# A retention layer and a two-matrix block on one core: unit 3 is loaded earlier and turned by the DMA queue, k and v come by halves from unit 4 on

## The chip, the cores and the metric

The kernel runs on one core of a Trainium2 chip. The core has a matrix engine (TensorE, PE in the profile; PEld is its weight load), a vector engine (VectorE, DVE), a scalar engine (ScalarE, ACT), a general engine (GpSimd, POOL) and a queue engine (SyncE, SP) that issues most transfers. Each engine runs its own instructions in the order in which they were written; semaphores hold an instruction back until what it reads is there. The metric is the device time of one execution in microseconds (us), the median of several runs.

## The reference

Eight heads (H = 8) of width 64 (D) are processed for four batches (B = 4) of 768 tokens (S). Per head a 64 by 64 state decays and takes in the outer product of k and v; a token's output is its q times the state:

```python
gamma = 1.0 - 2.0 ** (-5.0 - np.arange(H, dtype=np.float32))
scale = 1.0 / np.sqrt(D)
for t in range(S):
    state = gamma[None, :, None, None] * state + np.einsum('bhd,bhe->bhde', k[:, :, t], v[:, :, t])
    y[:, :, t] = scale * np.einsum('bhd,bhde->bhe', q[:, :, t], state)
...
h = x @ w_in            # x: y as 3072 tokens by 512; w_in 512 by 2048
g = np.maximum(h, 0.0) + alpha * np.minimum(h, 0.0)
return (g @ w_out).astype(np.float32)   # w_out 2048 by 512
```

Inputs and the output are 32-bit floats.

## The kernel before

**Units and blocks.** The 3072 tokens are cut into 12 units of 256 tokens (three per batch), and two units make a block of 512 tokens; there are six blocks. A unit holds two chunks of 128 tokens, which lie on two halves of 64 partitions with two tokens (r = 0 and 1) per partition.

**A unit's retention.** `load` brings k, q and v (1.5 MB in all) from memory with DMAs issued by SP. `rescale` multiplies k and q by decay factors into 16-bit numbers (on POOL or DVE), `cast_v` turns v into 16 bits. q and k are then needed transposed (`kq`): `turn_pe` does it with 8 PE transposes and one ScalarE copy for each half of the heads, `turn_dma` with one transposing DMA issued by SP. `score_mm` multiplies k with q into two PSUM banks, `masks` (DVE) multiplies with the causal mask, `sum_mm` and `state_sum` / `state_copy` carry the state (PE, DVE, POOL, with copies on POOL or ACT), and `out_mm` adds the state's part (line 319) and the masked part (line 339). `take_y` writes the unit's output as 16-bit numbers.

**Two layouts of k and v.** Below `SPLIT` (6 before) one DMA brings a whole k or v, partition p holding tokens 2p and 2p+1 of a chunk in rows of 512 bytes (line 149). From `SPLIT` on four DMAs bring k and four bring v (line 143), each in rows of 256 bytes, so that r = 0 is the first half of a 128-token chunk and r = 1 the second. Then the matmuls for r = 1 need only the later 64 of 128 columns, in the scores (line 284) and in the output (line 339), and a mask is 384 wide instead of 512 (line 297 instead of 301). q is loaded the same way in both.

**A block's two products.** `ffn1` multiplies the block with w_in on PE (line 407), ScalarE takes the negative part (line 418) and DVE combines the two (line 420). `ffn2` multiplies with w_out (line 445, block 0 only); from block 1 on `ffn2_seven` does it with seven instead of eight block products (line 493), from sums of w_out (`w_sums`, line 378, one wide instruction and six narrower ones, on DVE) and sums of g (`g_sums`, line 391, on DVE).

**Order.** There is no planner: the order is written out by hand. `ffn1` and `ffn2` are generators that yield after each matmul, and `tick(gen, m)` puts m matmuls of one of them between other work. In the stretch that the change touches, `gen` is `ffn2` of block 0 and `half` is `ffn1` of block 1, whose first half (48 ticks) needs only unit 2 and whose second half needs unit 3 too. Weights come in four pieces each, from POOL's queue (`get_wi`, `get_wo`). `hold` lets the next load of `load` wait for an instruction that was put into `held`. `behind` lets a rescale on POOL wait for the last `w_sums` or `g_sums` on DVE. Buffers of k, q, v, `kdq`, `kq` and `vx` are threefold. SP's queue carries loads, the transposing DMAs and the stores of the output in one order, and each waits for the one before it to be issued.

Of the kernel before, what the change touches and what calls it, by code (L numbers as in the profile page):

```python
# [21 lines left out]
def kernel(  # L22
# [15 lines left out]

    SPLIT = 6
    U = 256
    UPB = S // U
    NU = B * UPB
# [42 lines left out]
    HF, HM = NFT // 2, d_model // 2  # L87
# [15 lines left out]
    held = []  # L103

    def behind(ins, other):
        tc.add_manual_dep(
            ins.ins,
            other.ins.name,
            mybir.DependencyInfo(
                mybir.DependencyClass.Sync, mybir.DependencyReason.DATA  # L110
            ),
            reason="one engine of two at the second read port",
        )
# [52 lines left out]
    def rescale(eng, u, t, h0, h1):  # L166
        kdq = unit(u)[0]
        at = OQ if t else (O2 if u >= SPLIT else 0)
        return eng.tensor_tensor(  # L169
            out=kdq[:, t, :, h0:h1, :].rearrange("p r h d -> p h r d"),  # L170
            in0=staged[u]["kq"[t]][:, h0:h1, :].rearrange("p h (r d) -> p h r d", r=2),
            in1=tab[:, at + 2 * h0 : at + 2 * h1]
            .rearrange("p (h r) -> p h r", r=2)
            .unsqueeze(3)
            .to_broadcast([128, h1 - h0, 2, D]),
            op=MULT,
        )

    def cast_v(eng, u, h0=0, h1=H):
        o = unit(u)[2][:, h0:h1].rearrange("p h r d -> p (h r d)")  # L180
        i = staged[u]["v"][:, h0:h1].rearrange("p h x -> p (h x)")
        if eng is nc.scalar:
            eng.activation(out=o, in_=i, func=COPY, bias=0.0, scale=1.0)
        else:
            eng.tensor_copy(out=o, in_=i)  # L185
# [107 lines left out]
    def masks(u, hh, parts=(0, 1)):  # L293
        for a in parts:
            m2 = sbp.tile([128, 512], F16, tag=f"m2{a}{hh}", bufs=2, name=f"m2{a}{hh}")
            if u >= SPLIT:
                i = nc.vector.tensor_tensor(
                    out=m2[:, 0:384], in0=live[u, hh][a][:, 0:384], in1=mj, op=MULT
                )
            else:  # L300
                i = nc.vector.tensor_tensor(  # L301
                    out=m2.rearrange("p (r a i) -> p r a i", r=2, a=2),
                    in0=live[u, hh][a].rearrange("p (r a i) -> p r a i", r=2, a=2),
                    in1=mask.unsqueeze(2).to_broadcast([128, 2, 2, 128]),
                    op=MULT,
                )
            live[u, hh][a] = m2
        return i

    def out_mm(u, banks, evict=True):  # L310
        _, kq, vx = prepped[u]
        ys = [ps(banks[0], "y0"), ps(banks[1], "y1")]
        inter = [(u, c) in tgs for c in range(2)]
        assert inter == [u % UPB > 0, True]

        for c in range(2):
            for p in range(NP):
                if inter[c]:
                    nc.tensor.matmul(  # L319
                        out=ys[c][:, 128 * p : 128 * p + 128],  # L320
                        lhsT=tgs[u, c][:, p, :],
                        rhs=kq.rearrange("p (t r a) i -> p t r a i", t=2, r=2)[
                            :, 1, :, p, rows(c)
                        ],
                        start=(p == 0),
                        stop=False,
                        skip_group_check=True,
                    )
        for p in range(NP):
            m2s = live[u, p // 2]  # L330
            for r in range(2):
                for c in range(2):
                    for a in range(2):
                        o = ys[c][rows(a), 128 * p : 128 * p + 128]
                        at, n = 256 * r + 128 * (p % 2), 128
                        if u >= SPLIT and r == 1:
                            at, n = 256 + 64 * (p % 2), 64
                            o = o.rearrange("p (r i) -> p r i", r=2)[:, :, 32:64]
                        nc.tensor.matmul(  # L339
                            out=o,  # L340
                            lhsT=vx[rows(c), 2 * p + a, r, :],
                            rhs=m2s[a][rows(c), at : at + n],
                            start=(r == 0 and p == 0 and not inter[c]),
                            stop=(r == 1),
                            skip_group_check=True,
                        )
        live[u] = ys
        if evict:
            take_y(u, (0, 1))
# [20 lines left out]
    def w_sums(i, lo, hi):  # L370

        w = w_out_all.rearrange("p (k f) (j e) -> p k f j e", k=2, j=2)
        w12, w21, w22 = w[:, 0, lo:hi, 1, :], w[:, 1, lo:hi, 0, :], w[:, 1, lo:hi, 1, :]
        t1, t2, t3, t4 = (wsum[:, x, lo:hi, :] for x in range(4))
        o, a, b = (
            (t1, w12, w[:, 0, lo:hi, 0, :]), (t2, w22, t1), (t3, w22, w12), (t4, w21, t2)
        )[i]
        return nc.vector.tensor_tensor(out=o, in0=a, in1=b, op=SUB)
# [190 lines left out]
    def tick(gen, m=10**6):  # L569
        for _ in range(m):  # L570
            if next(gen, 1) == 1:
                return
# [8 lines left out]
    def get_wo(i):  # L581
        s = slice(4 * i, 4 * i + 4)
        return nc.gpsimd.dma_start(out=w_out_all[:, s, :], in_=wo[:, s, :])
# [88 lines left out]
    get_wo(1)  # L672
    rescale(G, 2, 1, 0, 4)
    rescale(G, 2, 0, 4, 8)
    rescale(G, 2, 1, 4, 8)
    cast_v(G, 2)
    out_mm(1, (4, 5), evict=False)
    take_y(1, (0,))
    take_y(1, (1,), V)
# [1 line left out]


    gen = ffn2(0, (0, 1, 2, 3), parts=4)
    half = ffn1(1, (6, 7, 4, 5, 4, 6, 0, 1, 2, 3, 0, 4, 5, 6, 7, 1), apart=12)
    tick(gen, 5)
    turn_pe(2, 0, 5)
    tick(gen, 5)
    score_mm(2, 0, (6, 7))
    held.append(masks(2, 0, (0,)))
    load(3, ("k0", "q0", "k1", "q1", "v"))  # L690
    masks(2, 0, (1,))
    turn_pe(2, 1, 4)
    tick(gen, 6)
    score_mm(2, 1, (6, 7))
    sum_mm(2, (5, 4))
    state(2, 0, G, "ga")
    masks(2, 1)
    held.append(get_wo(2))
    load(4)
    load(5)  # L700
    rescale(V, 3, 0, 0, 4)
    rescale(G, 3, 1, 0, 4)
    get_wo(3)
    rescale(V, 3, 0, 4, 8)
    rescale(G, 3, 1, 4, 8)
    cast_v(G, 3)
    w_sums(0, 0, HF)
    tick(gen, 9)
    out_mm(2, (4, 5))
    tick(gen, 7)  # L710
    tick(half, 24)
    turn_pe(3, 0, 6)
    tick(half, 8)
    turn_pe(3, 1, 7)
    tick(half, 16)
    tick(gen, 9)
    score_mm(3, 0, (4, 5))
    masks(3, 0)
# [7 lines left out]
    for f in (0, 4):  # L726
        for i in range(1, 4):
            gate = w_sums(i, f, f + 4)
    behind(rescale(G, 4, 1, 0, 8), gate)
    rescale(G, 5, 0, 0, 8)  # L730
    rescale(G, 5, 1, 0, 8)
    cast_v(G, 4)
    cast_v(G, 5)
    tick(gen, 8)
    out_mm(3, (6, 7))
    tick(gen)
# [6 lines left out]
    for n in range(1, NBLK):  # L743
        more = n + 1 < NBLK
        u0 = 2 * (n + 1)
        if n > 1:
            gen = ffn1(n, (7, 2, 3, 1, 0, 6, 5, 4, 7, 1, 0, 4, 5, 6, 7, 1))
            if more:
                for u in (u0, u0 + 1):
                    i = rescale(G, u, 0, 0, 8)  # L750
                    if u == u0:
                        behind(i, gate)
                    rescale(G, u, 1, 0, 8)
                    turn_dma(u)
                    cast_v(G, u)
                    if u + 2 < NU:
                        load(u + 2)
                    tick(gen, 8)
            tick(gen)
        gen = ffn2_seven(n, 0, 1) if more else ffn2_seven(n, (0, 3), 1, 2)  # L760
        if more:
            tick(gen, 8)
            sum_mm(u0, (2, 3))
            sum_mm(u0 + 1, (2, 3), half=1)
            score_mm(u0, 0, (4, 5))
            score_mm(u0, 1, (6, 7))
            state(u0, 0, G)
            masks(u0, 0)
            s01 = state_sum(u0, 1, G)
            masks(u0, 1, (0,))  # L770
            s10 = state_sum(u0 + 1, 0, G)
            masks(u0, 1, (1,))
            tick(gen, 8)
            state_copy(s01, "aa")
            state_copy(s10)
            tick(gen, 17)
            if n == 1:
                load(7)
            state(u0 + 1, 1, G)
            g_sums(n, 2, 0, HF)  # L780
            tick(gen, 15)
            out_mm(u0, (4, 5))
            score_mm(u0 + 1, 0, (6, 7))
            score_mm(u0 + 1, 1, (2, 3))
            masks(u0 + 1, 0)
            masks(u0 + 1, 1)
            gate = g_sums(n, 3, 0, HF)
            tick(gen, 32)
            out_mm(u0 + 1, (4, 5))
        else:  # L790
            tick(gen, 33)
            g_sums(n, 2, 0, HF)
            g_sums(n, 3, 0, HF)
        tick(gen)
# [30 lines left out]
```

## Time and profile before

The median is 202.07 us (three runs: 201.91, 202.07, 203.52). The profiled execution took 203.15 us.

| what | value |
|---|---|
| profiled execution, its span | 203.15 us, 201.4 us |
| PE busy, share of the span | 193.2 us, 96% |
| DVE busy | 155.3 us, 77% |
| ACT busy | 102.0 us, 51% |
| POOL busy | 85.1 us, 42% |
| granted clock of PE | full (1.00) |
| moved by DMA | 33.95 MB, mean 169 GB/s |

Busy time is what the profiler saw an engine work. A granted clock of 1.00 means that nothing slowed PE. A line of the timeline gives the start and the length in us, the engine, the line of the kernel, the operation, what it writes and reads, and how many instructions were merged; in brackets stands how long the engine sat idle before and who ended that.

### The profile page before, as it was taken

The page shows a single profiled execution, that of the slowest core. Times are in us where ns is not written, and L with a number is a line of the kernel's source. Part 1 is how long each engine was busy: PE and PEld are TensorE (multiplying, and loading weights), DVE is VectorE, ACT ScalarE, POOL GpSimd, SP SyncE. Part 2 cuts the span into 40 slices and gives each one's busy share as a digit, 9 for nine tenths or more (in the row PEclk, how much of TensorE's full clock was granted, in tenths as well). Part 3 has the DMA queues.
Part 4 walks back from the last instruction along what each step waited for, and adds up shares of the span by engine and source line. Part 5 has one row for each costly group of instructions (what it writes and reads, how often), then busy time and mean ns, then how long its engine had stood idle before and what let it go on. Part 6 is the DMA issues. An engine that isn't in the chain of part 4 may idle for free.

```text
span 201.4 us, 5574 instructions
## 1 busy us (share of the span) xinstructions
PE 193.2 (96%) x2325; PEld 129.0 (64%) x2325; DVE 155.3 (77%) x251; ACT 102.0 (51%) x170; POOL 85.1 (42%) x99
## 2 busy tenths in 40 slices
PE   6896999999999999999999999999999999999993
PEld 2455644577467778744788644788544888544882
DVE  7695887657799999189997389994489984589851
ACT  2455776348276433477354377334476255466321
POOL 6189029282459463970076950176920250000000
PEclk9999999999999999999999999999999999999999
DMA  6999999499999997998976499992570011300014
GB/s 170 312 230 148 205 251 260 136 245 198 339 344 136 215 222 180 240 277 221 213 188 162 157 178 240 198 225 87 175 160 0 3 53 55 107 0 0 14 41 156
DMA packets 77561, 33.95 MB, mean 169 GB/s; under 512 B 43217, under 2 KB 77025, under 8 KB 77537
## 3 DMA queue, kind: packets, MB, share of 16 engines
q1 hardware_dynamic: 73136, 29.37, 56.8%
q0 software_dynamic: 4224, 4.19, 13.4%
q8 instruction: 18, 0.29, 0.6%
q10 hardware_dynamic: 176, 0.04, 0.1%
q14 instruction: 7, 0.05, 0.1%
HBM read 27.31 MB, written 6.29 MB: 167 GB/s over the span
## 4 chain that ended last, share of the span: by engine, by line
PE 86%; DMA 6%; DVE 2%; POOL 2%; SPq 1%; issue 1%; ACT 0%; POOLq 0%
PE hps L407 41%; PE ox L493 16%; PE oy L493 11%; PE ops L445 7%; DMA win<-in_moe_w_in_dram 4%; PE y L339 3%; DMA vs<-in_v_dram 3%; PE y L319 2%; PE sca L284 2%; SPq L149 1%; PE st L229 1%; PE trb L199 1%; PE oz L493 1%; DVE gs L391 1%; POOL tf L255 1%
## 5 line engine op out<-in xcount | busy, mean ns | idle before, releaser
L407 PE MATMUL hps<-xT,win 128*128 128x512 f16 (+1 forms) x448 | 84.7, 349 | 1.6 <-DMA win<-in_moe_w_in_dram 1.6
L420 DVE SCALAR_TENSOR_TENSOR gt<-hm,oma,hps 128x512 f16<-128x512 f32 (+1 forms) x112 | 71.1, 668 | 10.2 <-ACT hm L418 4.9
L418 ACT ACTIVATE hm<-hps 128x512 f32<-128x512 f32 x96 | 57.2, 597 | 32.2 <-PE hps L407 29.7
L407 PEld LDWEIGHTS <-win 128*128 128x128 f16 x448 | 43.5, 98 | 40.2 <-DMA win<-in_moe_w_in_dram 1.7
L493 PEld LDWEIGHTS <-gs 128*128 128x128 f16 x320 | 31.0, 98 | 3.8
L255 POOL TENSOR_TENSOR tf<-ss,tab 128x256 f32<-128x256 f32 x16 | 12.2, 764 | 36.2 <-DVE ss L254 35.3
L493 PEld LDWEIGHTS <-gt 128*128 128x128 f16 x240 | 22.8, 98 | 4.6
L509 ACT ACTIVATE cu<-ox 128x512 f32<-128x512 f32 (+1 forms) x18 | 9.5, 527 | 29.3 <-PE ox L493 29.2
L169 POOL TENSOR_TENSOR kdq<-ks,tab 128x1024 f16<-128x1024 f32 (+1 forms) x10 | 17.3, 1729 | 15.6 <-DMA ks<-in_k_dram 8.4
L514 DVE TENSOR_TENSOR os<-oy,cu 128x512 f32<-128x512 f32 x14 | 9.6, 689 | 17.2 <-PE oy L493 13.5
L169 POOL TENSOR_TENSOR kdq<-qs,tab 128x1024 f16<-128x1024 f32 (+1 forms) x13 | 21.3, 1641 | 2.8 <-issue 1.9
L270 POOL CAST tg<-tf 64x256 f16<-64x256 f32 x27 | 13.2, 491 | 19.6 <-DVE tf L251 18.3
L493 PE MATMUL ox<-wsum,gs 128*128 128x256 f16 x160 | 19.1, 273 | 0.0
L362 ACT ACTIVATE xT<-y 128x512 f16<-128x512 f32 x23 | 15.7, 743 | 6.0 <-PE y L339 5.8
L445 PE MATMUL ops<-wout,gt 128*128 128x512 f16 x64 | 15.3, 380 | 0.0
L185 POOL CAST vx<-vs 128x1024 f16<-128x1024 f32 (+1 forms) x13 | 12.5, 971 | 4.1 <-DMA vs<-in_v_dram 4.1
L391 DVE TENSOR_TENSOR gs<-gt 128x1024 f16<-128x1024 f16 (+1 forms) x14 | 13.1, 934 | 0.3
L268 ACT ACTIVATE tg<-tf 64x256 f16<-64x256 f32 x13 | 5.3, 414 | 14.0 <-POOL tf L255 9.0
L205 ACT ACTIVATE kq<-trb 128x1024 f16<-128x1024 f16 x8 | 8.2, 1024 | 7.1 <-PE trb L199 7.0
L301 DVE TENSOR_TENSOR m<-sca,mi 128x512 f16<-128x512 f32 x12 | 8.2, 687 | 3.4 <-PE scb L284 3.4
L493 PE MATMUL ox<-wout,gt 128*128 128x256 f16 x80 | 10.4, 274 | 0.0
L445 PEld LDWEIGHTS <-gt 128*128 128x128 f16 x64 | 5.8, 98 | 6.0
(55 smaller groups left out, 190.7 us busy)
## 6 DMA issues: line engine op xcount, KB each, us to landing
out_dram<-os SPq DMA_DIRECT2D x21, 256.0 KB, 3.0
qs<-in_q_dram SPq DMA_DIRECT2D x8, 512.0 KB, 5.7
ks<-in_k_dram SPq DMA_DIRECT2D x24, 128.0 KB, 3.5
vs<-in_v_dram SPq DMA_DIRECT2D x24, 128.0 KB, 4.8
ks<-in_k_dram SPq DMA_DIRECT2D x8, 256.0 KB, 4.8
qs<-in_q_dram SPq DMA_DIRECT2D x8, 256.0 KB, 5.1
win<-in_moe_w_in_dram POOLq DMA_DIRECT2D x4, 512.0 KB, 7.8
wout<-in_moe_w_out_dram POOLq DMA_DIRECT2D x4, 512.0 KB, 8.1
```

Of the source, the lines that this page charges most:

```text
L169: return eng.tensor_tensor(out=kdq[:, t, :, h0:h1, :].rearrange("p r h d -> p h r d"), in0=staged[u]["kq"[t]][:, h0:h1, :].rearrange("p h ...
L185: eng.tensor_copy(out=o, in_=i)
L255: eng.tensor_tensor(out=t, in0=ss, in1=dec, op=MULT)
L270: nc.gpsimd.tensor_copy(out=o, in_=i)
L362: nc.scalar.activation(out=o, in_=i, func=COPY, bias=0.0, scale=1.0,)
L391: return nc.vector.tensor_tensor(out=o, in0=a, in1=b, op=op)
L407: nc.tensor.matmul(out=hps[:, f, :].rearrange("p (u t) -> p u t", t=U), lhsT=w_in_all[:, hp, 128 * (f0 + f) : 128 * (f0 + f) + 128], rhs=x ...
L418: nc.scalar.activation(out=hm, in_=hps, func=RELU, bias=0.0, scale=-1.0)
L420: nc.vector.scalar_tensor_tensor(out=gt[:, f0 + f, U * lo : U * hi], in0=hm[:, f, :], scalar=oma_sb[:, f0 + f : f0 + f + 1], in1=hps[:, f, :],
L445: nc.tensor.matmul(out=opss[tq], lhsT=gt[:, ft, 128 * tq : 128 * tq + 128], rhs=w_out_all[:, ft, :], start=(ft == 0), stop=(ft == NFT - 1),)
L493: nc.tensor.matmul(out=o[1][m], lhsT=lhs(f, m), rhs=rhs(f), start=(first and f == 0 and (m == 0 or o[0] is None)), stop=(f == HF - 1), ski ...
L514: nc.vector.tensor_tensor(out=so, in0=o[0], in1=t, op=ADD)
```

## The change

Six edits of the order of the program, and one number.

1. `SPLIT` goes from 6 to 4: units 4 and 5 load k and v by halves, with nine DMAs each instead of three, and use the narrower matmuls and masks.
2. Unit 3's loads are issued behind unit 2's last rescale (POOL) instead of behind unit 2's first mask (DVE). The third piece of w_out is issued right behind `cast_v` of unit 2, no longer later with the loads of unit 4 waiting for it.
3. Unit 3 is turned by `turn_dma` and not by two `turn_pe`; the loads of units 4 and 5 stand behind that in SP's queue.
4. The first 48 ticks of `half` run without a break, and its banks change with that.
5. The first, wide `w_sums` stands behind those ticks on DVE instead of ahead of them.
6. On POOL the casts of v of units 4 and 5 stand earlier among the rescales.
7. In the loop, the second mask of the second half of the heads stands ahead of the state's sum of the next unit.

```diff
-    SPLIT = 6
+    SPLIT = 4
...
-    rescale(G, 2, 1, 4, 8)
+    held.append(rescale(G, 2, 1, 4, 8))
+    load(3, ("k0", "q0", "k1", "q1", "v"))
     cast_v(G, 2)
+    get_wo(2)
...
-    half = ffn1(1, (6, 7, 4, 5, 4, 6, 0, 1, 2, 3, 0, 4, 5, 6, 7, 1), apart=12)
+    half = ffn1(1, (6, 7, 4, 5, 6, 7, 0, 1, 2, 3, 0, 4, 5, 6, 7, 1), apart=12)
...
-    held.append(masks(2, 0, (0,)))
-    load(3, ("k0", "q0", "k1", "q1", "v"))
-    masks(2, 0, (1,))
+    masks(2, 0)
...
-    held.append(get_wo(2))
-    load(4)
-    load(5)
     rescale(V, 3, 0, 0, 4)
     rescale(G, 3, 1, 0, 4)
     get_wo(3)
     rescale(V, 3, 0, 4, 8)
     rescale(G, 3, 1, 4, 8)
+    turn_dma(3)
+    load(4)
+    load(5)
     cast_v(G, 3)
-    w_sums(0, 0, HF)
     tick(gen, 9)
     out_mm(2, (4, 5))
     tick(gen, 7)
-    tick(half, 24)
-    turn_pe(3, 0, 6)
-    tick(half, 8)
-    turn_pe(3, 1, 7)
-    tick(half, 16)
+    tick(half, 48)
+    w_sums(0, 0, HF)
     tick(gen, 9)
     score_mm(3, 0, (4, 5))
...
+    cast_v(G, 4)
     behind(rescale(G, 4, 1, 0, 8), gate)
     rescale(G, 5, 0, 0, 8)
+    cast_v(G, 5)
     rescale(G, 5, 1, 0, 8)
-    cast_v(G, 4)
-    cast_v(G, 5)
...
             masks(u0, 1, (0,))
+            masks(u0, 1, (1,))
             s10 = state_sum(u0 + 1, 0, G)
-            masks(u0, 1, (1,))
```

## The prediction

> **What bounds the kernel now.** I read the page's busy shares first, then the chain that ended last, then PE's timeline around units 3 to 5, then SP's.
>
> ```profile
> span 201.4 us, 5574 instructions
> PE 193.2 (96%) x2325; PEld 129.0 (64%) x2325; DVE 155.3 (77%) x251; ACT 102.0 (51%) x170; POOL 85.1 (42%) x99
> PE 86%; DMA 6%; DVE 2%; POOL 2%; SPq 1%; issue 1%; ACT 0%; POOLq 0%
> ```
>
> PE carries the end: from 17.7 us on, when the first weights land, it has one idle stretch before its last matmul, and that is 0.43 us long. So a change is worth what it takes off PE's own work plus that stretch, less any new wait of PE. PE's timeline at the places touched:
>
> ```profile
> 45.52 0.62 PE L199 MATMUL trb<-mi,kdq 128*128 128x128 f16 x8
> 45.98 1.04 PE L407 MATMUL hps<-xT,win 128*128 128x256 f16 x8
> 46.85 0.61 PE L199 MATMUL trb<-mi,kdq 128*128 128x128 f16 x8
> 47.30 1.91 PE L407 MATMUL hps<-xT,win 128*128 128x256 f16 x16
> ...
> 66.87 1.04 PE L493 MATMUL ox<-wout,gt 128*128 128x256 f16 x8
> 74.72 0.41 PE L339 MATMUL y<-m,vx 64*64 64x128 f16 x15 [0.43 <-DVE m L301]
> 83.63 13.98 PE L407 MATMUL hps<-xT,win 128*128 128x512 f16 x64
> 156.25 1.07 PE L493 MATMUL ox<-wout,gt 128*128 128x256 f16 x8
> 171.99 1.24 PE L407 MATMUL hps<-xT,win 128*128 128x512 f16 x5
> ```
>
> See in it: the two groups of transposes of unit 3 (start to start 0.46 and 0.45 us), the one wait, and the same stretch of program twice. From the first `ox` of block 1 to the next block's `hps` (66.87 to 83.63) PE handles units 4 and 5 in the wide form; from 156.25 to 171.99 it handles units 10 and 11, which stand at the same places in their batch and run the same instructions, in the narrow form.
>
> SP's queue is what the change loads more:
>
> ```profile
> 47.78 0.37 SPq L149 DMA_DIRECT2D ks<-in_k_dram  x1
> 53.77 2.20 SPq L149 DMA_DIRECT2D vs<-in_v_dram  x1
> 59.05 0.62 SPq L459 DMA_DIRECT2D out_dram<-cu  x1
> 62.12 5.63 SPq L189 DMA_TRANSPOSE kq<-kdq  x2
> 67.84 2.75 SPq L143 DMA_DIRECT2D ks<-in_k_dram  x4
> 71.31 4.78 SPq L143 DMA_DIRECT2D vs<-in_v_dram  x4
> 76.80 2.66 SPq L143 DMA_DIRECT2D ks<-in_k_dram  x4
> 80.23 3.59 SPq L143 DMA_DIRECT2D vs<-in_v_dram  x4
> 95.56 2.84 SPq L189 DMA_TRANSPOSE kq<-kdq  x1
> 98.45 3.50 SPq L143 DMA_DIRECT2D ks<-in_k_dram  x4
> 102.67 4.63 SPq L143 DMA_DIRECT2D vs<-in_v_dram  x4
> ```
>
> Units 4 and 5 took 47.78 to 55.97 us to issue, whole. Halved loads take longer: unit 6 67.84 to 76.09 (8.25), unit 7 76.80 to 83.82 (7.02), unit 9 98.45 to 107.30 (8.85, the longest), unit 8 6.65 (the shortest).
>
> **The parts.**
>
> *Transposes on PE.* 16 leave the path: 0.46 + 0.45 = **0.91 us**. The two ScalarE copies (1.02 us each) lay beside PE.
>
> *Narrow units 4 and 5, and the moved mask.* The twin stretches give it at once: 16.76 us (83.63 - 66.87) against 15.74 us (171.99 - 156.25), so **1.02 us**. The 0.43 us wait is in that. I check that the wait can go: DVE's masks took 0.685 us and take 0.547 narrow (groups by form), so the four of unit 4 end 0.55 us sooner; the one that PE waited for also no longer stands behind a state's sum (0.33 us in the queue, and 0.22 us idle for POOL's product before it). It was 0.43 us late; it is then some 0.6 us early. The state's sum that now stands behind it feeds `out_mm` of unit 5 at 79.0 us, over 4 us later. In later blocks the same swap fills a DVE idle of 0.33 us (102.87) off the path.
>
> *Unit 3's loads.* Held behind POOL's last rescale of unit 2, which ends at 33.91, they start 2.75 us sooner than at 36.69. They now meet the rest of w_out's second piece (landed 36.1) and the third piece, issued at about 34.9. In the trace k's and q's second halves landed 6.0 and 6.7 us after the first issue; unit 2's loads beside weights took 10.4 and 11.2. The nearest row is the former, with a third piece also in flight, so I take 8 us for q's second half, landing near 42.0 (bounds 40.6 and 45.1). POOL, freed of the third piece's issue (0.81 us), rescales the first half of q at 40.1 and issues the fourth piece at 41.1, then rescales the second half by 43.1 us (1.04 us; it took 1.92 beside the wide `w_sums`, which moves away). Nothing on PE waits for a load here but through the next part.
>
> *The DMA turn of unit 3.* Issued at 43.1; the eight in the trace took 3.7 to 6.3 us to land, so kq is there at 46.8 to 49.4. PE wants it at 51.1 - 0.9 = 50.2. Cost nothing: 48 steps of `half` and nine of `gen` (42.9 to 51.1 us before) stand in front and hide it. If q lands at 45.1, the turn lands at up to 52.5, and PE waits 2.3 us. The fourth piece of w_out, wanted at about 52.5, landed 8.4 us after issue: 49.5.
>
> *Loads of units 4 and 5.* They stand behind that turn on SP, whose issue takes 1.3 to 2.8 us: start near 45.4, not 47.78. I take 8.25 + 7.02 = 15.3 us for the pair, the rows of the first pair behind a turn (bounds 13.3 and 17.7, twice the shortest and twice the longest). SP is done at 60.7. Behind that stand four stores (0.33 to 0.62 us when not held: 1.7 in all), so unit 4's turn is issued at 62.4, against 62.12 before; its rescale, gated by `w_sums`, is done at about 61.2 and is not last. It landed in 5.6 us before, others behind stores in 4.4 and 4.7; with 5.0 kq is there at 67.4. PE wants it (score of unit 4, 68.29 before) at 68.29 - 0.91 = 67.4. So the wait is about 0, and between -2.5 (turn issued at 61.2, landed in 3.7) and +3.7 us (17.7 for the pair, landed in 6.3) at the ends. I put **0.2 us** on the path, because the estimate sits on the edge and only lateness counts.
>
> [...]
>
> *v and the rest on SP.* v of unit 5 lands some 4.2 us after its last issue, near 64; its cast ends at 65.1, wanted at 66.9. The rescale of q behind it ends at 67, 1.2 us later than before, and unit 5's turn lands by 73, about when PE wants it (73.3, by the twin stretch). Unit 6's loads start 1 to 1.5 us later; in the stores ahead of unit 6's turn (83.92 to 86.44, they waited for DVE) there is that much room. Unit 7's turn landed at 101.9, PE wants it at 104.7 - 1.9 = 102.8. Cost nothing.
>
> *The wide sum and the casts.* `w_sums` (1.22 us) moves to about 49.6 on DVE, where before it had idle gaps of 0.52 and 0.84 us; the masks of unit 3 start 0.2 us behind PE, caught up in the second gap. POOL's cast of unit 4 (1.03 us) falls beside the last sums; beside POOL work such sums took 0.88 to 1.10 instead of 0.68 us, so up to 0.8 us is added on DVE. The sum that PE needs next, `gs` of block 1, ended at 70.97 and was wanted at 71.54: 0.57 us of slack. Cost 0 to 0.3; I take 0, as the ten last steps of `half` let DVE catch up (its 0.75 us a step on the last four against PE's 0.87).
>
> **Sum.** -0.91 - 1.02 + 0.2 = -1.73 us: the profiled execution would take 203.15 - 1.73 = 201.4. That one ran 1.08 us over the median; on the median's scale 202.07 - 1.73 = **200.3 us**, 0.86% less. About 1% (2 us) is what a measurement of this kernel can tell from no change.
>
> **Rivals.**
>
> *Unit 4's turn is late.* The loads of units 4 and 5 run as unit 6's and unit 9's did (17 us), or the first turn starts a microsecond late. PE waits 0.6 to 1.9 us at the first score of unit 4: 200.7 to 202.1. For it: the estimate has no margin, and before there was only 0.6 us (landed 67.7, wanted 68.29). Against it: the loads start 2.4 us sooner. Chance 0.25.
>
> *Slower: halves drag the whole queue.* Same place, decided by the pair's time: PE waits for 52.1 + P - 67.4, so from P = 17.2 us on the whole gain is gone, and at 17.7 with a turn of 6.3 us behind a backlog (as at 95.56) the wait is 3.7: 203.8. If the pair also shares the rings with w_out's fourth piece, still 0.5 MB, P reaches 19 and the time 205. Against it: no pair in the trace took more than 15.5. Chance 0.15, 0.09 of it over 1%.
>
> *Unit 3's turn is the late one.* q's second half lands at 45.1 as beside weights: PE waits up to 2.3 us at the first score of unit 3, and everything after shifts with it, so that unit 4's turn then costs little more: 201 to 202.6. Chance 0.1.
>
> *The change gives all of it.* No new wait at all: 200.1, and below 200.05 (over 1%) with a noise of 0.1 to 0.2 us. The forecast with its 0.2 us and this case together hold 0.5, of which 0.24 lies below 200.05.
>
> **How the numbers follow.** The forecast's own range is 199.8 to 200.7 (0.5); rivals reach on: to 202.1 (0.25), 202.6 (0.1) and 205 (0.15). Leaving 0.05 below and 0.12 above, the range is 199.8 to 203.0. Faster by over 1%: 0.27, with a little for waits that I overrate. Slower by over 1%: 0.1. Within: 0.63.
>
> **What would show it.** Right: no line 199 after 37 us; PE's stretch of block 1 close to 15.7 us; no wait on PE for the masks of unit 4. Unit 3's turn on SP near 43, landed before 50; loads of units 4 and 5 ending near 60.7; unit 4's turn landing near 67.4. Wrong: PE idle ahead of line 284 at 50 or 67 us, or ahead of line 493 at 70 us for `gs`, or SP still issuing halves after 62 us.

## The result, and the profile after

The changed kernel takes 207.49 us (median of six runs, 206.42 to 208.44) against 202.22 us (six runs of the kernel before, 201.91 to 203.52): a ratio of 1.0251, with a 95% interval of 1.0204 to 1.0298. It is slower. The forecast of 200.3 us and its whole range, up to 203.0, miss it. The profiled execution after took 207.50 us. Here and below a median is that of all executions of a kernel, while a ratio leaves out those that ran in a slower state, so the two need not agree.

The page of the kernel after, its span, busy times and the engines' shares of the chain that ended last:

```profile
span 205.8 us, 5554 instructions
PE 192.6 (94%) x2309; PEld 127.5 (62%) x2309; DVE 154.8 (75%) x251; ACT 100.3 (49%) x168; POOL 84.7 (41%) x99
PE 76%; DMA 11%; DVE 7%; POOL 2%; issue 1%; ACT 1%; SPq 1%; DVEq 0%
```

PE does less (192.6 us after 193.2, 16 instructions fewer) in a longer span, and its share of the chain falls from 86% to 76%, while DMA's rises from 6% to 11%. So the work went, and waits came. PE's timeline of the kernel after says which:

```profile
42.03 3.66 PE L407 MATMUL hps<-xT,win 128*128 128x256 f16 x32
46.41 1.92 PE L407 MATMUL hps<-xT,win 128*128 128x256 f16 x16 [0.72 <-DVE gt L420]
48.16 2.11 PE L445 MATMUL ops<-wout,gt 128*128 128x512 f16 x9
52.90 0.24 PE L284 MATMUL sca<-kq 64*64 64x128 f16 x1 [2.63 <-DMA kq<-kdq]
...
53.53 1.90 PE L445 MATMUL ops<-wout,gt 128*128 128x512 f16 x8
...
59.99 3.66 PE L407 MATMUL hps<-xT,win 128*128 128x256 f16 x32
64.53 5.37 PE L407 MATMUL hps<-xT,win 128*128 128x256 f16 x32 [0.88 <-DVE gt L420]
69.74 1.04 PE L493 MATMUL ox<-wout,gt 128*128 128x256 f16 x8
...
73.58 0.24 PE L284 MATMUL sca<-kq 64*64 64x128 f16 x1 [2.18 <-DMA kq<-kdq]
...
87.81 4.48 PE L407 MATMUL hps<-xT,win 128*128 128x512 f16 x20
```

No line 199 stands here any more, and no wait of line 339. In their place are four waits, 6.41 us together: two for a unit's turned q and k (2.63 us at unit 3, 2.18 us at unit 4) and two for DVE's combining of block 1 (0.72 and 0.88 us). Laying the same starts of both timelines side by side gives the whole difference of the spans:

| stretch of PE's program (start before, start after) | longer by |
|---|---|
| up to the first `hps` of block 1 (42.89, 42.03) | -0.86 us |
| its first half, with or without the transposes (to 49.04, 48.16) | -0.02 us |
| unit 3's first scores (to 51.71, 53.53) | +2.70 us |
| to the second half of block 1's `hps` (to 58.17, 59.99) | 0.00 us |
| that half (to 66.87, 69.74) | +1.05 us |
| units 4 and 5 (to 83.63, 87.81) | +1.31 us |
| everything up to the last 16 `ox` (to 196.31, 200.49) | 0.00 us |
| end of the span | +0.2 us |
| sum (201.4 to 205.8) | +4.4 us |

The first row is no part of the change: PE's first `hps` waited 1.57 us for w_in in the execution before and 0.27 us in this one, where PE's weight load waited 0.43 us for the first piece of w_out at 31.7 us. Without that row the change costs 5.2 us, which is what the medians say (207.49 - 202.22 = 5.27). The narrow stretch shows the saving plainly: 18.07 us after less its wait of 2.18 is 15.89, where 15.74 was expected and 16.76 stood before.

SP's queue of the kernel after tells why both turns were late:

```profile
34.97 0.37 SPq L149 DMA_DIRECT2D ks<-in_k_dram  x1
...
36.94 0.50 SPq L149 DMA_DIRECT2D qs<-in_q_dram  x1
37.48 0.51 SPq L149 DMA_DIRECT2D vs<-in_v_dram  x1
46.80 3.35 SPq L189 DMA_TRANSPOSE kq<-kdq  x1
50.20 2.74 SPq L143 DMA_DIRECT2D ks<-in_k_dram  x4
...
60.73 3.25 SPq L143 DMA_DIRECT2D vs<-in_v_dram  x4
64.08 0.62 SPq L459 DMA_DIRECT2D out_dram<-os  x1
...
66.40 6.53 SPq L189 DMA_TRANSPOSE kq<-kdq  x2
72.98 2.65 SPq L143 DMA_DIRECT2D ks<-in_k_dram  x4
```

Unit 3's turn is issued at 46.80, not near 43, and lands 6.1 us later, at 52.9. The queue then runs behind the plan: the halves of units 4 and 5 start at 50.20 instead of 45.4 and end at 63.98, four stores follow, and unit 4's turn is issued at 66.40 and lands 7.1 us later, at 73.5, where PE wanted it at 71.4. The pair of loads itself took 13.8 us, less than the 15.3 forecast.

POOL's timeline of the kernel after shows what unit 3's turn waited for:

```profile
35.91 0.80 POOL L583 DMA_DIRECT2D wout<-in_moe_w_out_dram  x1
...
43.69 1.04 POOL L169 TENSOR_TENSOR kdq<-qs,tab 128x512 f16<-128x512 f32 x1 [4.57 <-DMA qs<-in_q_dram]
44.67 0.80 POOL L583 DMA_DIRECT2D wout<-in_moe_w_out_dram  x1
45.74 1.03 POOL L169 TENSOR_TENSOR kdq<-qs,tab 128x512 f16<-128x512 f32 x1 [0.27 <-DMA qs<-in_q_dram]
```

q's second half landed at 45.66 us, 10.7 us after the first issue. And DVE's timeline of the kernel after shows the other two waits:

```profile
44.88 0.69 DVE L169 TENSOR_TENSOR kdq<-ks,tab 128x512 f16<-128x512 f32 x1 [5.18 <-DMA ks<-in_k_dram]
45.49 4.78 DVE L420 SCALAR_TENSOR_TENSOR gt<-hm,oma,hps 128x256 f16<-128x256 f32 x12
...
57.36 1.67 DVE L378 TENSOR_TENSOR wsum<-wout,wsum 128x1024 f16<-128x1024 f16 x1
...
61.57 1.52 DVE L378 TENSOR_TENSOR wsum<-wout 128x1024 f16<-128x1024 f16 x1
63.01 0.68 DVE L378 TENSOR_TENSOR wsum<-wout,wsum 128x1024 f16<-128x1024 f16 x1
63.62 6.89 DVE L420 SCALAR_TENSOR_TENSOR gt<-hm,oma,hps 128x256 f16<-128x256 f32 x15
```

DVE sat idle for 5.18 us on the second half of k, and the combining steps (`gt`) that free PE's banks stand behind that rescale: 0.72 us on PE. Later two of the sums of w_out, 0.69 and 0.68 us in the kernel before, took 1.67 and 1.52 us: the first beside POOL's rescale of unit 4's k, which began at 56.58, just after the last of that k had landed (56.41), the second beside POOL's cast of v, which now stands there. The six sums took 6.33 us, against 4.51 before (55.54 to 60.05); the `gt`s behind them start that much later, and PE waits 0.88 us.

### The profile page after: what moved, and what is told of

Its sections match the earlier page's. It is cut to its first block, busy times and chain, and to the rows that moved or that the text cites. A ratio compares the mean times of both kernels' runs of the same rounds, so it can differ in the third digit from the quotient of the medians.

```text
span 205.8 us, 5554 instructions
## 1 busy us (share of the span) xinstructions
PE 192.6 (94%) x2309; PEld 127.5 (62%) x2309; DVE 154.8 (75%) x251; ACT 100.3 (49%) x168; POOL 84.7 (41%) x99
## 4 chain that ended last, share of the span: by engine, by line
PE 76%; DMA 11%; DVE 7%; POOL 2%; issue 1%; ACT 1%; SPq 1%; DVEq 0%
PE hps L407 34%; PE ox L493 17%; PE oy L493 12%; DMA kq<-kdq 6%; DMA vs<-in_v_dram 5%; DVE wsum L378 3%; DVE m L301 3%; PE kps L96 2%; PE y L339 2%; PE ops L445 2%; PE sca L284 2%; PE y L319 2%; PE st L229 1%; PE oz L493 1%; PE trb L199 1%
## 5 line engine op out<-in xcount | busy, mean ns | idle before, releaser
L420 DVE SCALAR_TENSOR_TENSOR gt<-hm,oma,hps 128x512 f16<-128x512 f32 (+1 forms) x112 | 70.2, 666 | 8.7 <-ACT hm L418 3.7
L255 POOL TENSOR_TENSOR tf<-ss,tab 128x256 f32<-128x256 f32 x16 | 11.5, 717 | 33.3 <-DVE ss L254 32.8
L169 POOL TENSOR_TENSOR kdq<-qs,tab 128x1024 f16<-128x1024 f32 (+1 forms) x13 | 20.4, 1570 | 6.8 <-DMA qs<-in_q_dram 5.5
L270 POOL CAST tg<-tf 64x256 f16<-64x256 f32 x27 | 14.1, 522 | 21.3 <-DVE tf L251 20.0
L445 PE MATMUL ops<-wout,gt 128*128 128x512 f16 x64 | 15.3, 380 | 0.1
L284 PE MATMUL sca<-kq 64*64 64x128 f16 (+1 forms) x192 | 7.5, 211 | 5.9 <-DMA kq<-kdq 4.8
L284 PEld LDWEIGHTS <-kq 64*64 64x64 f16 x384 | 5.6, 107 | 9.2 <-DMA kq<-kdq 5.4
L493 PE MATMUL ox<-wout,gt 128*128 128x256 f16 x80 | 10.4, 274 | 0.0
```

Source lines behind the costliest of these rows:

```text
L169: return eng.tensor_tensor(out=kdq[:, t, :, h0:h1, :].rearrange("p r h d -> p h r d"), in0=staged[u]["kq"[t]][:, h0:h1, :].rearrange("p h ...
L255: eng.tensor_tensor(out=t, in0=ss, in1=dec, op=MULT)
L270: nc.gpsimd.tensor_copy(out=o, in_=i)
L284: nc.tensor.matmul(out=scs[a][rows(c), at : at + n], lhsT=kv[rows(a), 0, r, p, rows(c)], rhs=q, start=True, stop=True,)
L420: nc.vector.scalar_tensor_tensor(out=gt[:, f0 + f, U * lo : U * hi], in0=hm[:, f, :], scalar=oma_sb[:, f0 + f : f0 + f + 1], in1=hps[:, f, :],
L445: nc.tensor.matmul(out=opss[tq], lhsT=gt[:, ft, 128 * tq : 128 * tq + 128], rhs=w_out_all[:, ft, :], start=(ft == 0), stop=(ft == NFT - 1),)
```

## Experiments

The ratios are against the kernel before, run beside each kernel on the same chip. The first five undo or move one part of the change in the kernel after; the others, but for one whose heading says so, put parts into the kernel before or test a rival there. The question of the first group is which of the four waits decides, and whether the turns are late because of the weights in flight, of the halves, or of POOL's and DVE's order.

### The third piece of w_out back where it was (kernel after)

```diff
     cast_v(G, 2)
-    get_wo(2)
...
     masks(2, 1)
+    get_wo(2)
     rescale(V, 3, 0, 0, 4)
```

> The changed kernel with w_out's third piece issued where it was before (after unit 2's last masks, on POOL), everything else as changed. Theory 1 (the third piece shares the rings with unit 3's loads and makes them late): q's second half lands about 7 us after the first load is issued instead of 10.7, PE's waits of 0.72 us at 46.4 and 2.63 us ahead of unit 3's scores shrink to under 0.5 together, unit 4's turn is issued 3 us sooner and its wait of 2.18 us falls under 1: 202.5 to 203.5 us. Theory 2 (the turn by the queue and the halved loads are slow by themselves, the weights do not matter): the waits stay within 1 us of what they were, 206.5 to 207.5.

Measured: 207.76 us, ratio 1.0269 (1.0225 to 1.0313), no faster. The loads did recover: first issue at 34.01, q's second half landed at 40.4, 6.4 us after it instead of 10.7, and the 0.72 us wait went. But the third and the fourth piece now stand close together on POOL, and both are in flight when the turn is issued. PE's timeline of this kernel:

```profile
52.03 0.24 PE L284 MATMUL sca<-kq 64*64 64x128 f16 x1 [2.03 <-DMA kq<-kdq]
...
72.03 0.31 PE L284 MATMUL sca<-kq 64*64 64x128 f16 x1 [2.43 <-DMA kq<-kdq]
...
72.82 1.89 PE L493 MATMUL ox<-wout,gt 128*128 128x256 f16 x8
74.50 2.35 PE L493 MATMUL oy<-wout,gt 128*128 128x256 f16 x16
```

The turn is issued at 44.24 and lands 7.7 us later, and PE waits 2.03 and 2.43 us. So the third piece did slow unit 3's loads, as expected of it, but moving it back passes the delay on to the turn. A second cost shows in the last two lines: `ox` x8 takes 1.89 us where it took 1.05 in the kernel after. The same kernel by stretches (busy us of each engine, then the granted clock, the DMA share and GB/s):

```profile
72.00:73.00 1.00, 0.97 (x33) 0.85 (x34) 0.76 (x3) 0.00 (x0) 0.55 (x1) 0.50 1.27 290
73.00:74.00 1.00, 1.00 (x6) 0.75 (x5) 1.00 (x4) 0.00 (x0) 0.85 (x3) 0.50 0.73 163
74.00:75.00 1.00, 1.00 (x7) 0.69 (x6) 1.00 (x3) 0.26 (x1) 0.61 (x1) 0.50 0.81 183
75.00:76.00 1.00, 1.00 (x9) 0.82 (x8) 0.22 (x1) 0.96 (x3) 0.61 (x1) 0.81 0.68 155
```

From 71.98 us, just before PE resumes, its clock is granted at 0.50 for some 3.4 us. Half of that, about 1.7 us, is by estimate lost on top of the wait; measured, the stretch of units 4 and 5 without its wait took 17.45 us here and 15.89 in the kernel after, 1.56 us more.

### Units 4 and 5 whole again (kernel after)

```diff
-    SPLIT = 4
+    SPLIT = 6
```

> The changed kernel with units 4 and 5 loaded whole and multiplied wide again (the boundary back at 6). Theory 1 (halved loads hold up SP, so that unit 4's turn is late): the two loads take 8 us of SP instead of 13.8, PE's wait of 2.18 us ahead of unit 4's scores goes, PE's own work grows by about 0.6 us: near 205.9. Theory 2 (that wait is only carried on from unit 3's late turn): the wait stays, 207.5 to 208.1. The waits around unit 3 stay by both.

Measured: 203.94 us, ratio 1.0028 (0.9988 to 1.0068). SP's queue in this kernel:

```profile
45.38 2.79 SPq L189 DMA_TRANSPOSE kq<-kdq  x1
48.22 0.57 SPq L149 DMA_DIRECT2D ks<-in_k_dram  x1
...
54.07 1.45 SPq L149 DMA_DIRECT2D vs<-in_v_dram  x1
...
62.73 6.32 SPq L189 DMA_TRANSPOSE kq<-kdq  x2
```

The six loads are issued in 7.3 us instead of 13.8, the turn of unit 4 lands 3.7 us after its issue, and its wait is gone. Only unit 3's wait is left (1.75 us). The gain, 2.2% or 4.5 us by the ratios, is more than that wait, although the narrow matmuls' saving is given up, and the expectation had less. The rest of it is in the other waits: the 0.72 and the 0.88 us are not in this profile either. The first depends on the moment: here, and in the experiment with the casts below, q's second half landed some 10.1 us after the first issue, at 44.2 in both, and DVE had the second half of k 1.3 and 1.4 us sooner than in the profile after. For the second see the experiment with the casts: the cast stands early here too.

### Unit 3 turned by PE (kernel after)

```diff
-    rescale(G, 3, 1, 4, 8)
-    turn_dma(3)
+    held.append(rescale(G, 3, 1, 4, 8))
...
-    tick(half, 48)
+    tick(half, 24)
+    turn_pe(3, 0, 6)
+    tick(half, 8)
+    turn_pe(3, 1, 7)
+    tick(half, 16)
```

The banks of `half` are those of the kernel before, as those transposes need them.

> The changed kernel with unit 3 turned by PE again (two groups of transposes among the 48 ticks, banks as before), the loads of units 4 and 5 held behind unit 3's last rescale so that they start when the queue's turn would have been issued. Theory 1 (late loads of unit 3 and then the 6 us of the queue's turn make PE wait): the wait of 2.63 us goes, 0.91 us of transposes comes, SP is free 3.4 us sooner so that unit 4's wait falls to about 0.5: near 204.1. Theory 2 (unit 3's scores wait for its loads however it is turned): PE waits at the transposes instead, 206.5 or more.

Measured: 202.29 us, ratio 0.9977 (0.9945 to 1.001). With the turn off SP, k of unit 4 goes out from 37.12 on (`hold` holds q only, not the four DMAs of a halved k), SP is done with unit 5 at 59.4, unit 4's turn is issued at 62.74, and PE waits for no `kq`. Left are 0.27 and 0.39 us for `gt`. That is more than was expected (204.1). With the turn off SP's queue the whole loss is gone, and with whole loads behind the turn nearly all of it was, so it takes both: the turn in the queue, and halves held back behind it that unit 4's turn then meets. As k of unit 4 also goes out 13 us sooner here, this run does not tell the turn's own wait from what it holds back.

### The casts of v back behind the rescales (kernel after)

```diff
-    cast_v(G, 4)
     behind(rescale(G, 4, 1, 0, 8), gate)
     rescale(G, 5, 0, 0, 8)
-    cast_v(G, 5)
     rescale(G, 5, 1, 0, 8)
+    cast_v(G, 4)
+    cast_v(G, 5)
```

> The changed kernel with POOL's casts of v of units 4 and 5 back behind the rescales. The 0.88 us that PE waits at 64.5 for DVE (the small sums of w_out took 1.67 and 1.52 us beside POOL instead of 0.68) should go by both theories. Theory 1 (the turn of unit 4, which SP issues late, sets the end of this stretch): the wait ahead of unit 4's scores grows by as much, no change, 207.3 to 207.7. Theory 2 (DVE's sums set it): 206.6.

Measured: 208.01 us, ratio 1.0297 (1.024 to 1.0354). The wait of 0.88 us is gone, and the sum of w_out that took 1.52 us takes 0.68. But PE still waits 1.78 and 2.07 us for the two turns, and behind the second the clock stands at 0.50 from 70.8 to 74.3. So the time does not hang on the 0.88 us: with PE earlier, it waits for the turn instead. Nor did the cast cause the 0.88 us alone: with units 4 and 5 whole it stands early too, and PE waited for no `gt`. Here the first sum too took 0.68 us, not 1.67, so this run does not part the two long sums.

### The fourth piece of w_out behind unit 3's cast (kernel after)

```diff
-    get_wo(3)
     rescale(V, 3, 0, 4, 8)
...
     cast_v(G, 3)
+    get_wo(3)
```

> The changed kernel with w_out's fourth piece issued behind the cast of unit 3's v instead of between the two rescales of unit 3's q. Theory 1 (a weight piece in flight slows the queue's turn of unit 3, which landed in 6.1 and 7.7 us beside one and two pieces and in 3.7 with none): that turn lands within 4.8 us of its issue and PE's wait ahead of unit 3's scores falls from 2.63 to under 1.2 us; PE then waits up to 1.5 us for the late piece instead: 205.5 to 207.5. Theory 2 (the turn takes some 6 us behind any load): the landing and the wait stay within 0.5 us, and with the wait for the piece it is over 207.5.

Measured: 209.89 us, ratio 1.0351 (1.03 to 1.0402). PE's waits in this kernel:

```profile
55.74 0.38 PE L445 MATMUL ops<-wout,gt 128*128 128x512 f16 x1 [3.82 <-DMA wout<-in_moe_w_out_dram]
...
74.95 0.24 PE L284 MATMUL sca<-kq 64*64 64x128 f16 x1 [2.44 <-DMA kq<-kdq]
```

No weights are in flight now when unit 3's turn is issued (45.25), and it lands in 3.8 us; the wait ahead of unit 3's scores is gone. PE waits for the piece itself instead, 3.82 us, and runs at half clock from 57 to about 60.4 us; and unit 4's turn is later still, so that the time is above what the first theory allowed. Together with the runs above this orders the landing of unit 3's turn of 512 KB by the pieces of w_out in flight when it is issued: 3.8 us with none, 5.5 (twice) to 6.1 us with one, 7.7 us with two.

### The halves alone (kernel before)

```diff
-    SPLIT = 6
+    SPLIT = 4
```

> The kernel before with the boundary at 4 and nothing else. Theory 1 (halves hold up SP): its two loads take about 14 us of SP from 47.8 on, the stores follow, unit 4's turn is issued at 63.5 instead of 62.1 and lands some 6 us later, PE waits about 1.1 us against 1.02 saved on PE: 201.5 to 203, and up to 1.7 us more where PE's clock drops to half after the wait. Theory 2 (halves cost nothing by themselves): 201.2.

Measured: 206.11 us, ratio 1.015 (1.0092 to 1.0207). The halves make the kernel slower by themselves, and by more than was expected; k of unit 4 also goes out at 38.24 and not at 47.8, as `hold` does not hold it. SP's queue in this kernel:

```profile
38.24 7.32 SPq L143 DMA_DIRECT2D ks<-in_k_dram  x4
47.44 0.38 SPq L149 DMA_DIRECT2D qs<-in_q_dram  x1
47.91 5.87 SPq L143 DMA_DIRECT2D vs<-in_v_dram  x4
...
57.28 3.10 SPq L143 DMA_DIRECT2D vs<-in_v_dram  x4
...
62.81 6.18 SPq L189 DMA_TRANSPOSE kq<-kdq  x2
```

k of unit 4 meets the third and fourth piece of w_out, which land in 8.4 and 10.4 us; the loads end at 60.4 instead of 55.97; the turn is issued at 62.81 and lands in 6.4 us. This execution started earlier by 0.8 us than the one of before that was shown; the kernel with only the moved mask, which started as early, issues that turn at 60.98. PE waits 1.83 us for it at 69.29, and the clock is at 0.50 from 70.7 to 74.1. That is more than the narrow stretch saves.

### The same DMAs with rows of 512 bytes (kernel before)

k and v of units 4 and 5 come in four DMAs each, cut by pairs of heads and not by tokens; the layout and the matmuls stay wide.

```diff
+            if u in (4, 5) and nm != "q":
+                for g in range(4):
+                    hg = slice(2 * g, 2 * g + 2)
+                    nc.sync.dma_start(
+                        out=t[nm[0]][:, hg, :],
+                        in_=src[b, hg, U * c : U * c + U, :].rearrange(
+                            "h (p r) d -> p h (r d)", r=2
+                        ),
+                    )
+                continue
```

> The kernel before (boundary at 6, wide form) with k and v of units 4 and 5 brought in four DMAs each, two heads at a time, so that SP issues nine DMAs for each unit as with halves but with rows of 512 bytes. It is set beside the kernel with halves alone, where SP ended these loads at 60.4 and PE waited 1.83 us for unit 4's turn. Theory A (the number of DMAs that SP issues costs): SP ends within 1 us of 60.4, unit 4's turn is late by 1 us or more, 203.5 or more. Theory B (the short rows cost on the DMA engines): SP ends before 59, no wait over 0.3 us, within 0.3% of before.

Measured: 202.81 us, ratio 1.004 (1.0011 to 1.0069). SP's queue in this kernel:

```profile
38.20 3.78 SPq L151 DMA_DIRECT2D ks<-in_k_dram  x4
48.09 0.37 SPq L159 DMA_DIRECT2D qs<-in_q_dram  x1
48.56 2.29 SPq L151 DMA_DIRECT2D vs<-in_v_dram  x4
...
54.72 2.07 SPq L151 DMA_DIRECT2D vs<-in_v_dram  x4
```

The same four issues of k take 3.78 us where halves took 7.32, and four of v 2.29 where halves took 5.87. The loads end at 56.8, unit 4's turn is issued at 61.15, and PE waits for no `kq`. So the number of DMAs costs little, 0.4% (0.1 to 0.7); the short rows cost the rest of the 1.5%. In the stretch from 56 to 62 us the rings move 336 GB/s here and 235 GB/s with halves (some of it stores here), and from 52 to 58 us, where loads make up most of it, 285 and 175.

### The moved mask alone (kernel before)

```diff
             masks(u0, 1, (0,))
+            masks(u0, 1, (1,))
             s10 = state_sum(u0 + 1, 0, G)
-            masks(u0, 1, (1,))
```

> The kernel before with only the state's sum of the next unit moved behind the second mask. PE's wait of 0.43 us for that mask goes and nothing else changes: 0.2% less by both theories.

Measured: 201.99 us, ratio 0.996 (0.9922 to 0.9998). PE's stretch of units 4 and 5 in this kernel:

```profile
65.73 1.04 PE L493 MATMUL ox<-wout,gt 128*128 128x256 f16 x8
...
72.69 0.67 PE L339 MATMUL y<-m,vx 64*64 64x128 f16 x32
...
81.98 2.32 PE L407 MATMUL hps<-xT,win 128*128 128x512 f16 x10
```

All 32 of line 339 run as one group, without the wait of 0.43 us, and the stretch takes 16.25 us instead of 16.76. Of the parts tried alone in the kernel before, this is the one that pays.

### The moved mask, and halves loaded as early as SP can (kernel before)

The mask as above and `SPLIT = 4`; the loads of units 4 and 5 are released by unit 3's last rescale, ahead of all its scores, and no longer by the third piece of w_out:

```diff
-    held.append(get_wo(2))
-    load(4)
-    load(5)
+    get_wo(2)
...
-    rescale(G, 3, 1, 4, 8)
+    held.append(rescale(G, 3, 1, 4, 8))
+    load(4)
+    load(5)
```

> The kernel before (unit 3 turned by PE, its loads and the third piece where they were) with the moved mask, the boundary at 4, and the loads of units 4 and 5 released by unit 3's last rescale instead of by the third piece of w_out. Theory 1: they start at 45.5, end at 59.5 on SP, unit 4's turn lands before PE wants it, and the 1.02 us of the narrow form are kept: 0.5% less than before. Theory 2 (halves and the weight pieces together make w_out's third piece or unit 4's turn late): no gain, within 0.2%, or slower.

Measured: 204.16 us, ratio 1.0054 (1.0009 to 1.01). The loads still end at 61.9, the turn is issued at 65.21 and lands in 4.7 us, and PE waits 2.09 us at 69.99. The clock stays at 1.00. An earlier release of q does not help: k goes out unheld, at 38.55, beside w_out's pieces, its four DMAs hold SP for 7.58 us, and q follows only at 46.23.

### The moved mask, and halves for unit 5 only (kernel before)

```diff
-    SPLIT = 6
+    SPLIT = 5
```

with the mask as above.

> The kernel before with the moved mask and only unit 5 by halves (boundary at 5). SP's loads end 1.5 to 2.5 us later, which unit 4's turn, waiting for its rescale until 61, has room for; PE saves some 0.2 us in unit 5's scores and output: 0.1% under the moved mask alone, which was 0.4% under before. Rival: that room is not there, PE waits for unit 4's turn by 0.5 us or more and the gain of the moved mask is gone.

Measured: 202.07 us, ratio 0.9982 (0.996 to 1.0003). Unit 4's turn, issued at 64.82, causes no wait in the profiled execution, but that one had lost 2.39 us at its start waiting for w_in, so PE came later than usual and this profile shows little of the wait. By the times, halves of one unit gain nothing over the mask alone.

### Unit 3 turned by PE and the casts back (kernel after)

The edits of the third and the fourth experiment together.

> The changed kernel with unit 3 turned by PE and POOL's casts back behind the rescales: two of the seven edits undone. PE's wait of 0.39 us at 61.6 in the kernel with the PE turn alone came from the small sums beside POOL's cast and should go. If so: 0.4% less than before. Rival: the wait has another source (unit 3's rescale of k standing late in DVE's queue): 0.2% less, as without this edit.

Measured: 202.5 us, ratio 1.0014 (0.9979 to 1.0048). The 0.39 us wait for `gt` is gone, but in this profile PE waits 2.52 us at 46.55, ahead of unit 3's second transposes, for a `gt`: the second halves of q and k of unit 3 landed some 11 us after their issue beside the halves of unit 4 and the third piece, and DVE's rescale of k stood ahead of the `gt`s, as in the kernel after. No gain over turning by PE alone.

### The moved mask again (kernel before)

> The same kernel as the one with the moved mask alone, for a second set of runs, as its interval came close to no change. If the wait that goes (0.43 us) is all of it: 0.2% less. If the first 0.4% stands: the interval stays under 1.

Measured: 201.57 us (12 runs, 201.29 to 203.26), ratio 0.9968 (0.9938 to 0.9999). Twice some 0.3 to 0.4% under the kernel before, both intervals just below 1. It has the lowest ratio of the kernels tried, though the intervals of two others (unit 3 turned by PE, halves for unit 5 only) overlap with it.

## Why the prediction was wrong, step by step

**PE's own work: right.** The transposes went (line 199 is gone; 0.91 us), and the stretch of units 4 and 5 without its new wait is 15.89 us against the twin's 15.74. The old wait of 0.43 us left as argued, and the moved mask alone takes it (16.25 us).

**"Unit 3's loads": wrong row.** Of two rows, 6.7 us and 11.2 us, I took the first as the nearer and added a little: 8 us. With the same five loads and the third piece of w_out in flight it measured 10.1 to 11.1 in four profiles (kernel after, second, fourth and fifth experiment), and 6.4 without that piece (the first). The row of loads beside weights was the nearest, and the piece is issued by the very edit. The loads also started 1 us later than I put them (34.97 for 33.91). The text also said that nothing on PE waits for a load but through the turn. DVE's rescale of k is ahead of the `gt`s in its queue, so a late k stopped PE by 0.72 us; I had listed what waits behind POOL's and SP's instructions and not what waits behind DVE's.

**"The DMA turn of unit 3. Cost nothing": the step that failed first.** Its upper bound (q at 45.1, landing by 52.5, 2.3 us) was just passed: q at 45.66, landing at 52.9, 2.63 us. The landing times of 3.7 to 6.3 us were taken as scatter, but for this turn they sort by load, as the runs with none, one and two pieces of w_out in flight show. That the fourth piece is issued just ahead of the turn should have put it at the upper end.

**"Loads of units 4 and 5": the landing of the turn was mis-sized.** The pair took 13.8 us, below the 15.3 forecast, so the slower rival as I priced it (a pair of 17.2 us or more) did not happen. It started 4.8 us late behind unit 3's turn, and unit 4's turn was issued 4.0 us late (66.40 for 62.4). PE wanted it 4.0 us late as well (71.4 for 67.4), so that I had the shift right: "everything after shifts with it". The term that failed is the next one, "with 5.0": it landed in 7.1 us, and the difference of 2.1 is the wait of 2.18. I took the rows of turns behind stores and not the row of a backlog, 6.3 us. Right behind halves and stores the turn landed in 6.1 to 7.7 us (kernel after, first, fourth and fifth experiment), and in 3.7 behind whole loads that had ended 7 us earlier (the second). Company in the rings is not all of it, though: behind whole loads it took 5.5 to 5.6 us in the kernel before and with the moved mask, and in the kernel before the rings moved only 16, 145, 0 and 34 GB/s in the four us from 62 to 66, while it was under way; behind halves loaded early it took 4.7. What else holds up unit 4's turn is not shown. So two turns were late, each by its own landing, and I had made rivals of them that exclude each other.

The halves' own danger was real all the same: alone in the kernel before they cost 1.5%. The price is that of short rows, as the comparison with as many DMAs of 512-byte rows shows (ratios of 1.004 against 1.015). In the same stretch, 56 to 62 us, the rings moved 235 GB/s with rows of 256 bytes and 336 with rows of 512, stores included. I had given the slower rival 0.15, because no pair of loads in the trace was long enough; what is still in the rings behind the halves was not in that sum (from 62 to 64 us they moved 354 and 399 GB/s with the halves alone, 16 and 145 in the kernel before, unit 4's turn, issued at 62.81 and 62.12, included).

**"The wide sum and the casts: I take 0": wrong in size.** The bound was 0.8 us more on DVE; the six sums took 1.8 us more, and PE waited 0.88 us. A sum took 1.52 to 1.67 us beside POOL's work, not the 1.10 of the row I used. The slack I looked at was that of the sum; the `gt`s behind it had less. Undoing it gains nothing while the turns are late.

**What was missed altogether: the clock.** Waits of PE were priced at their length. In five of the profiles of experiments the clock fell to 0.50 for some 3.4 us late in a wait or up to 1.43 us behind it, by estimate worth about 1.7 us more (half of 3.4; 1.56 measured with the third piece back); the profiled execution of the kernel after does not show it, so it is not part of the 4.4 us above. By the runs' means the clock was lower in others of that kernel: those at a mean clock of 0.983 took 208.41 and 208.44 us, one at 0.992 took 207.47, those at 0.998 to 0.999 took 206.42 to 207.50. Why the profiled one, with waits of 2.63 and 2.18 us, lost nothing is not shown.

**The sum.** Forecast -1.73 us on the profiled execution; measured +4.35, of which -0.86 is the start. The terms that differ are the four waits (6.41 us against 0.2) and the start; what is left, some 0.7 us, is small delays, 0.17 us in the first and again in the second half of block 1 among them.

## What to carry to other kernels

When transfers are moved earlier, sum each queue as a chain and let the rivals along it add up: each transfer that PE waits for can be late for a reason of its own. Take the landing time of a DMA from rows with the same company in the rings, weights in flight above all (unit 3's turn: 3.8 us with no piece in flight, 7.7 with two). Leave room for a long wait of PE to cost more than its length: with five waits here, of 1.83 to 3.82 us, came some 3.4 us at a clock of 0.50, with eight others, of 1.75 to 2.63 us, none. Weigh narrower matmuls against the shorter rows of a load that they need: here 1 us of PE work was bought with some 3.5 us of waiting and slow clock (the halves alone: 1.83 us of wait, and by estimate 1.7 of slow clock).

## What the runs showed of the hardware

- In five profiles the granted clock fell to 0.50 for some 3.4 us late in a wait of PE or shortly behind it:

| run | wait of PE, and when it ended | the clock fell at |
|---|---|---|
| third piece back | 2.43 us, 72.03 | 71.98 us |
| casts back | 2.07 us, 70.35 | 70.84 us |
| fourth piece later | 3.82 us, 55.74 | 56.99 us |
| halves alone | 1.83 us, 69.29 | 70.72 us |
| halves for unit 5 | 2.39 us, 18.70 | 18.17 us |

- With eight other waits it stayed at 1.00: 2.63 and 2.18 us (kernel after), 2.03 us (third piece back, unit 3), 1.75 us (units 4 and 5 whole), 1.78 us (casts back, unit 3), 2.44 us (fourth piece later, unit 4), 2.09 us (moved mask and early halves) and 2.52 us (PE turn and casts back). So in these profiles the length of a wait alone does not tell: one of 1.83 us came with a fall, one of 2.63 us with none. What decides is not shown.
- One turn of 512 KB within the chip's own memory landed in 3.7 us (unit 4's, units 4 and 5 whole) and 3.8 us (unit 3's, fourth piece later) at the quickest, and in 7.7 us both beside two weight pieces (unit 3's, third piece back) and right behind halves and stores (unit 4's, fourth piece later).
- A 16-bit sum of 128x1024 on DVE (0.68 us) took up to 1.67 us beside POOL's rescale of k and 1.52 us beside its cast of v (kernel after).
- Four DMAs of 128 KB in rows of 256 bytes held SP for 5.87 and 7.32 us (halves alone), where four of the same size at the same places of the program in rows of 512 bytes held it for 2.29 and 3.78 us.
